# A token-mixing kernel: one PSUM tile for the transposition of x, chunks that enter over seven steps, and final channel mixes at other places

## The chip, the cores and the metric

The kernel runs on one core of a Trainium2 chip. The metric is the time of one execution on the device in microseconds (us). The core has five engines that work side by side, each in the order of its own instructions: TensorE (PE) for matmuls, VectorE (DVE), ScalarE (ACT), GpSimd (POOL), and SyncE (SP), which here only issues DMAs. ACT and POOL issue DMAs too. SBUF is the working memory, PSUM the memory into which PE writes.

## The reference

Two layers follow each other. The inputs are x (8 batches, 4224 tokens, 192 channels, float32), eight sets of seven taps, two token-mixing matrices of 4224 x 4224 and two channel-mixing matrices of 192 x 192.

```python
# layer 1: a causal convolution over 7 tokens, its taps softmaxed, one set per group of 24 channels
w = softmax(weight)                                  # [8 heads, 7 taps]
x = einsum('hk,bskhg->bshg', w, windows_of_7(x))     # [8, 4224, 192]

# layer 2
theta = x @ w_theta
zr, zi = x * cos(theta), x * sin(theta)
y = einsum('ts,bsd->btd', w_tok_r, zr) + einsum('ts,bsd->btd', w_tok_i, zi)
u = x + y
return u + maximum(u @ w_ch, 0)
```

By far the most work is y: two products of a 4224 x 4224 matrix with 4224 x 1536 numbers (8 batches of 192 channels).

## The kernel before

**Chunks and token blocks.** The 4224 source tokens are cut into 33 chunks k of 128, the 4224 target tokens into 33 blocks tb of 128. A unit is a pair of blocks (the seventeenth unit is a single block). For a pair the two products are done by a scheme of seven runs (`runs`, L394) on sums and differences of the matrices (S1 to S4) and of zr and zi (Z11, T1, Z21, Z22, T2, T4, T3). A run is two matmuls per chunk (L427). The sums of the matrices are formed by DVE (`turn`, L325, transposes the tiles that arrive from DRAM; `wsum`, L333). After a run `give` (L383) adds the result from PSUM to the row buffers `pv` of the unit; this is done by DVE (L392), and in the first pass by ACT for four of the seven (L390). The PSUM tiles of the runs (`y`) have two buffers.

**Steps.** SBUF holds eleven chunks (`zpool`). A step t treats one unit with all chunks that are there. A chunk stays for 17 steps, so that it meets each unit once; then a new chunk takes its place one step later. `base` (L64) says in which step each of the eleven slots begins, `start` (L66) the step in which each chunk begins. As slots begin at different steps, a step has between 2 and 11 chunks (`n`); one step is 0.324 x n x 7 us of PE work (`time`, L300), 24.9 us for a pair with eleven chunks. Between passes the sums are kept in DRAM (`part`): SP loads them into `pv` (`load_rows`, L356; six buffers shared with the input of chunks) and stores them at the end of the step (L440).

**What makes a chunk.** `Chunk.tasks` (L255): two convolutions as matmuls (`conv`, L192) evacuated by ACT; the transposition of x by PE in two halves of six 128 x 128 transposes (`transpose`, L221, `transposed`, L157), each into one bank of a PSUM tile of two banks, evacuated to the SBUF tile `uT` by ACT or DVE; two theta products with sine and cosine by ACT (`theta`, L229); products and sums by DVE. Convolutions, transposes and thetas share two PSUM tiles of two banks (`banks`, L109). The first eleven chunks are made in a loop at the start (L645 to L689), in which `between(n)` puts up to n pairs of token-mixing matmuls between the tasks, as far as their chunks are ready. The later ones are made within steps: each task has a place in units of a seventh of a step (`pos`, L528), the second chunk of one step begins 2.3 units after the first.

**The end.** In the last 17 steps (`final`) each block is finished: `add_x` (L367) has added x before (POOL, L374, or a DMA that accumulates in DRAM, L379, for the late steps and the first two of the final ones), ACT casts u to half precision (`cast`, L444), u is transposed, and `output` (L461) does the channel mix on PE (eight matmuls for a half of the columns, L138), takes the maximum and adds on DVE (L464), and stores the result (SP, L469). In final steps with all eleven chunks ("full") the transposition is a DMA on ACT's queue (`cross_u`, L458, L155). In those with fewer ("late") it is done by PE (`turn_u`, L453). `outputs` (L474) lists at which time after the end of its step, in us of token-mixing work, each of these is put into the order.

**Order.** The order on PE, DVE, ACT and POOL is written out by hand: the events of a step are sorted by their place and issued when `mix` (L414) gets there, and the helpers `pe`, `dve`, `act`, `pool` keep each engine to that order. SP's DMAs, and POOL's that are not wrapped in `pool`, are placed by a scheduler.

Of the kernel before, what the change touches and what calls it, by code (L numbers as in the profile page):

```python
# [16 lines left out]
def kernel(  # L17
# [23 lines left out]
    nc = tc.nc  # L41
# [3 lines left out]
    P = nc.NUM_PARTITIONS  # L45
# [11 lines left out]
    NG = B // GB  # L57
    GC = GB * D
# [2 lines left out]
    NW = 11  # L61
    PC = 512

    base = [0, 0, 1, 1, 2, 3, 3, 4, 4, 5, 5]  # L64
    assert len(base) == NW
    start = [base[k % NW] + (NU + 1) * (k // NW) for k in range(NK)]  # L66
    NSTEP = start[-1] + NU
# [13 lines left out]
    def pe(ins):  # L81
        return in_order("pe", ins)

    def dve(ins):
        return in_order("dve", ins)
# [58 lines left out]
    def evacuate(out, in_, by_dve=False):  # L144
        if by_dve:
            dve(nc.vector.tensor_copy(out=out, in_=in_))
        else:
            act(nc.scalar.activation(out=out, in_=in_, func=AT.Copy))  # L148

    def turned():  # L150
        return wk.tile([P, 12, P], F16, name="uT", tag="uT")
# [2 lines left out]

        act(nc.scalar.dma_start(out=uT, in_=u, transpose=True))  # L155

    def transposed(uT, u, by_dve=False):  # L157
        tp = banks("tp", F16)
        for k in range(6):
            pe(nc.tensor.transpose(  # L160
                tp[:, 0, k * P : (k + 1) * P], u[:, k * P : (k + 1) * P], ident
            ))
        evacuate(uT.rearrange("p k s -> p (k s)"), tp[:, 0, 0 : 6 * P], by_dve)

    Z11, T1, Z21, Z22, T2, T4, T3 = range(7)

    class Chunk:
# [50 lines left out]
                        out=xs[t0 : t0 + Q, :], in_=self.x[a * Q : (a + 1) * Q, :]  # L218
                    )

        def transpose(self, g):  # L221
            if g == 0:
                self.xT = turned()
            transposed(
                self.xT[:, 6 * g : 6 * g + 6, :], self.x[:, g * GC : (g + 1) * GC],
                0 < self.k < 3 or (self.k, g) == (0, 1),
            )

        def theta(self, g):  # L229
            v = channel_mix(self.xT[:, 6 * g : 6 * g + 6, :], wth).rearrange(  # L230
# [24 lines left out]
        def tasks(self):  # L255

            for j in range(2):
                yield lambda j=j: self.conv(j)
            for g in range(NG):
                yield lambda g=g: self.transpose(g)  # L260
            for g in range(NG):
                yield lambda g=g: self.theta(g)
            yield lambda: self.product(Z11)
            yield lambda: self.product(Z21)
            yield lambda: self.sums(0)
            yield lambda: self.sums(1)
# [13 lines left out]
    class Step:  # L280
# [170 lines left out]
            ))  # L451

        def turn_u(self, i, g):  # L453
            transposed(
                self.uT[i][:, 6 * g : 6 * g + 6, :], self.ub[i][:, g * GC : (g + 1) * GC]
            )

        def cross_u(self, i):  # L458
            crossed(self.uT[i], self.ub[i])
# [14 lines left out]
        def outputs(self):  # L474

            found = []
            for i in range(len(self.tbs)):
                if not self.late:
                    at = (4 if i else 0.9 - self.time / 7) if self.pair else 0.7
                    for g in range(NG):  # L480
                        found.append((at + g, lambda i=i, g=g: self.cast(i, g)))
                        found.append((at + 10.5 + 2.8 * g,
                                      lambda i=i, g=g: self.output(i, g)))
                    found.append((at + 2, lambda i=i: self.cross_u(i)))
                    continue
                at = 1.2 if i or not self.pair else 0.6 - self.time / 7
                every, turn, mix = 2.0, 1.2, 3.6
                for g in range(NG):
                    found.append((at, lambda i=i, g=g: self.cast(i, g)))
                    found.append((at + turn, lambda i=i, g=g: self.turn_u(i, g)))  # L490
                    found.append((at + mix, lambda i=i, g=g: self.output(i, g)))
                    at += every
            return found
# [7 lines left out]
    def step_events(t):  # L501
        found = []
        s = steps[t]
        if t + 1 < NSTEP:
            found += steps[t + 1].w_tasks()
            found.append((1.6, steps[t + 1].load_rows))
            if not steps[t + 1].ahead:
                for i in steps[t + 1].adds:
                    found.append((3.3 + 1.7 * i, lambda i=i: steps[t + 1].add_x(i)))
        for s in steps[t:]:  # L510
            if s.ahead and t == s.t - (4 if s.late else 10):
                for i in s.adds:
                    found.append((3.3 + 1.7 * i, lambda s=s, i=i: s.add_x(i)))
        if t + 2 < NSTEP:
            nxt = steps[t + 2]
            for m in (1, 2):
                found.append((1.3 + 3 * (m - 1), lambda m=m: nxt.load_w(m)))
        for at, f in outputs:
            begin = at - sum(s.time for s in steps[:t])
            if 0 <= begin < steps[t].time:  # L520
                found.append((7 * begin / steps[t].time, f))
        if t >= NU - 2:
            new = [k for k in range(NK) if start[k] == t + 2 and k >= NW]
            for k in new:
                found.append((4.5, lambda k=k: load_chunk(k)))
            at = 0.1
            for k in (k for k in range(NK) if start[k] == t + 1 and k >= NW):
                pos = [0, .5, 1.3, 1.6, 2.1, 2.5, 3.1, 3.15, 3.4, 3.6]  # L528

                def add(at, j, k):  # L530
                    def go():
                        if j == 0:
                            chunks[k].todo = chunks[k].tasks()
                        next(chunks[k].todo)()
                    found.append((at, go))
                for j, p in enumerate(pos):
                    add(at + p, j, k)
                at += 2.3
        return found
# [105 lines left out]
    for i in range(NW + 2):  # L645
        ch = chunks.get(i) if i < NW else None
        old = chunks[i - 1] if 0 < i <= NW else None

        def between(n):
            left = more(n)  # L650
            if 0 < i < 3:
                idle(min(left, 2))

        if ch:
            ch.conv(0)
        between(2)
        if old:
            old.theta(0)
        between(1)
        if ch:  # L660
            ch.conv(1)
        if i == 0:
            idle(4)
        ready[0] = i - 2
        between(2)
        if old:
            old.theta(1)
        if i == 1:
            for _, f in steps[0].w_tasks():
                f()  # L670
        if i + 3 < NW:
            load_chunk(i + 3)
        between(1)
        if ch:
            ch.transpose(0)
        if old:
            old.product(Z11)
        between(1)
        if ch:
            ch.transpose(1)  # L680
        if old:
            old.product(Z21)
        between(1)
        if old:
            old.sums(0)
        between(1)
        if old:
            old.sums(1)
        between(1)  # L689
    nc.vector.memset(wch[:, 1:3, :], 0.0)  # L690
    for rows, i, part_w in channel_pieces(moe_w_ch):
        nc.gpsimd.dma_start(out=wch[rows, i, :], in_=part_w)
    ready[0] = NK
# [33 lines left out]
```

## Time and profile before

| what | value |
|---|---|
| median of 5 runs | 1480.63 us |
| the five runs | 1466.3, 1472.12, 1480.63, 1482.14, 1494.6 us |
| the profiled execution: its time, its span | 1477.73 us, 1476.0 us |
| granted TensorE clock, mean | 0.991 |
| L427, token-mixing matmuls | 7656, 1292.8 us |
| L138, channel-mixing matmuls (theta and output) | 1056, 109.9 us |
| L160, transposes of x and of u on PE | 396 and 108, 42.0 us |
| L148, ACT evacuations of transposes | 79, 814 ns each |
| L392, DVE additions | 324, 951 ns each |
| L155, DMA transposes of u | 24, issue to landing 3.2 to 25.7 us, median 6.8 |
| DMA, mean over the span | 191 GB/s |

The span is the time from the first to the last instruction of the profiled execution. A group of instructions is named by its line, its engine, and what it writes and reads (`v<-wch,uT`). Busy time is the sum over its instructions; idle time in front of a group is given with what ended it. The chain that ended last is followed back from the end, from each piece of work to what released it. Busy times of engines overlap, so they do not add up to the span.

### The profile page before, as it was taken

Reading aid. Unit: us, or ns where it says so; the run is one execution under the profiler, and the core shown is the slowest. Engines: PE = TensorE matmul, PEld = TensorE weight load, DVE = VectorE, ACT = ScalarE, POOL = GpSimd, SP = SyncE. Lnnn points to the kernel's source line nnn. Section 1 sums busy time; section 2 is a strip of 40 time slices with the busy share of each in tenths; the row PEclk is TensorE's granted clock in tenths of the full one; section 3 lists DMA queues with packets and bytes.
Section 4 is the critical chain, followed back from the end, with each engine's and each line's share of the span. In section 5 each row is a group of like instructions: output and inputs, shape, how many; then the busy total and the mean of one; then the engine's idle time right before and its main releaser. Section 6 shows DMA issues by size and latency. Waiting matters only on the chain.

```text
span 1476.0 us, 23773 instructions
## 1 busy us (share of the span) xinstructions
PE 1421.2 (96%) x9807; PEld 887.2 (60%) x9807; DVE 1016.6 (69%) x1050; ACT 322.8 (22%) x413; POOL 434.8 (29%) x655
## 2 busy tenths in 40 slices
PE   7889999999999999999999999999999999996997
PEld 4556666666666666656656566666656666664665
DVE  6884554555458687777767758768778787774675
ACT  6861111111134353000000005245001101100034
POOL 7422211111223322522413333332123123233210
PEclk9999999999999999999999999999999999998999
DMA  9976756464699999987977799999898989999983
GB/s 176 225 161 145 143 100 147 94 150 92 156 225 229 213 214 274 205 224 163 244 166 215 173 196 240 187 240 262 152 201 191 212 195 239 207 249 154 246 219 118
DMA packets 272029, 281.98 MB, mean 191 GB/s; under 512 B 106673, under 2 KB 240177, under 8 KB 271921
## 3 DMA queue, kind: packets, MB, share of 16 engines
q0 software_dynamic: 162464, 92.15, 47.5%
q1 hardware_dynamic: 71824, 178.88, 34.7%
q10 hardware_dynamic: 37632, 9.44, 5.0%
q8 instruction: 77, 1.26, 0.3%
q14 instruction: 32, 0.25, 0.1%
HBM read 245.49 MB, written 108.13 MB: 240 GB/s over the span
## 4 chain that ended last, share of the span: by engine, by line
PE 84%; DVE 6%; DMA 4%; ACT 3%; issue 2%; POOL 0%; DVEq 0%; SPq 0%; ACTq 0%
PE y L427 75%; PE v L138 5%; DMA uT<-ub 3%; DVE wt L339 2%; PE pc L200 2%; ACT z L240 2%; DVE pv L392 1%; PE tp L160 1%; DVE wt L327 1%; DVE z L251 1%; DVE z L245 1%; ACT uT L148 1%; DVE pv L464 1%; ACT pv L390 0%; DMA xw<-in_x_dram 0%
## 5 line engine op out<-in xcount | busy, mean ns | idle before, releaser
L427 PE MATMUL y<-z,wt 128*128 128x384 f16 x7656 | 1292.8, 327 | 12.8 <-DVE pv L392 11.9
L427 PEld LDWEIGHTS <-wt 128*128 128x128 f16 x7656 | 740.7, 98 | 489.7 <-issue 16.4
L392 DVE TENSOR_TENSOR pv<-y,pv 128x768 f32<-128x768 f32 x324 | 308.1, 951 | 306.4 <-PE y L427 267.1
L327 DVE STREAM_TRANSPOSE wt<-st 128x1408 f16<-128x1408 f16 (+7 forms) x224 | 327.5, 1464 | 44.1 <-PE y L427 36.2
L314 POOL DMA_DIRECT2D st<-in_moe_w_tok_i_dram x232 | 132.4, 579 | 510.1 <-DVE wt L327 495.3
L314 POOL DMA_DIRECT2D st<-in_moe_w_tok_r_dram x232 | 132.5, 580 | 455.3 <-DVE wt L327 441.8
L339 DVE TENSOR_TENSOR wt<-wt 128x1408 f16<-128x1408 f16 (+7 forms) x216 | 218.5, 1012 | 45.6 <-PE y L427 43.4
L148 ACT ACTIVATE z<-pc 128x768 f16<-128x768 f32 x65 | 52.8, 813 | 390.5 <-PE pc L200 390.5
L449 ACT ACTIVATE ub<-pv 128x768 f16<-128x768 f32 x66 | 52.5, 836 | 361.3 <-DVE pv L392 321.6
L138 PEld LDWEIGHTS <-uT 128*128 128x128 f16 x1056 | 91.5, 98 | 40.7 <-DMA uT<-ub 17.3
L390 ACT ACTIVATE pv<-y 128x768 f32<-128x768 f32 x66 | 53.6, 813 | 282.8 <-PE y L427 282.7
L464 DVE SCALAR_TENSOR_TENSOR pv<-v,pv 128x768 f32<-128x768 f32 x66 | 62.7, 951 | 34.1 <-PE v L138 32.1
L187 POOL DMA_DIRECT2D xw<-in_x_dram x132 | 76.2, 587 | 29.7 <-DMA xw<-xw 5.9
L374 POOL TENSOR_TENSOR pv<-pv,xr 128x1536 f32<-128x1536 f32 x24 | 74.8, 3116 | 10.1 <-issue 9.3
L148 ACT ACTIVATE uT<-tp 128x768 f16<-128x768 f16 x79 | 63.0, 814 | 63.1 <-PE tp L160 62.2
L251 DVE TENSOR_TENSOR z<-z 128x768 f16<-128x768 f16 x132 | 73.3, 555 | 3.8
L138 PE MATMUL v<-wch,uT 128*128 128x192 f16 x528 | 54.9, 248 | 17.4 <-DMA uT<-ub 15.5
L240 ACT ACTIVATE z<-v,half_pi 128x768 f16<-128x768 f32 x66 | 59.5, 901 | 43.0 <-PE v L138 42.7
L245 DVE TENSOR_TENSOR z<-z 128x1536 f16<-128x1536 f16 x66 | 60.3, 948 | 9.9 <-ACT z L240 9.9
L138 PE MATMUL v<-wth,uT 128*128 128x192 f16 x528 | 55.0, 248 | 3.0 <-ACT z L240 2.8
L240 ACT ACTIVATE z<-v 128x768 f16<-128x768 f32 x66 | 53.1, 805 | 0.0
L160 PE MATMUL tp<-ident,z 128*128 128x128 f16 x396 | 33.1, 220 | 8.5 <-ACT z L240 8.0
(43 smaller groups left out, 147.4 us busy)
## 6 DMA issues: line engine op xcount, KB each, us to landing
part<-pv SPq DMA_DIRECT2D x79, 768.0 KB, 4.1
pv<-part SPq DMA_DIRECT2D x79, 768.0 KB, 5.8
out_dram<-pv SPq DMA_DIRECT2D x66, 384.0 KB, 5.5
st<-in_moe_w_tok_r_dram POOLq DMA_DIRECT2D x136, 176.0 KB, 5.5
st<-in_moe_w_tok_i_dram POOLq DMA_DIRECT2D x136, 176.0 KB, 5.0
xs<-z SPq DMA_DIRECT2D x132, 96.0 KB, 4.4
xw<-in_x_dram POOLq DMA_DIRECT2D x121, 96.0 KB, 5.9
xr<-xs SPq DMA_DIRECT2D x24, 384.0 KB, 4.6
```

What stands on the lines that cost most here:

```text
L138: pe(nc.tensor.matmul(v[:, k, b * D : (b + 1) * D], lhsT=tT[:, 3 * k + b + i, :], rhs=w[:, 2 * b + i, :], start=(i == 0), stop=(i == 1),))
L148: act(nc.scalar.activation(out=out, in_=in_, func=AT.Copy))
L187: nc.gpsimd.dma_start(out=self.xw[lo : lo + n, h, :, :], in_=x[:, t0 : t0 + n, :].rearrange("b s d -> s b d"),)
L240: act(nc.scalar.activation(**args))
L245: dve(nc.vector.tensor_tensor(out=o, in0=xv, in1=o, op=ALU.mult))
L251: dve(nc.vector.tensor_tensor(out=z[:, o, :], in0=z[:, a, :], in1=z[:, b, :], op=ALU.subtract))
L314: pool(nc.gpsimd.dma_start(out=st[a * Q : (a + 1) * Q, 0:nb, :, 0:n] .rearrange("i r bt s -> i (r bt) s"), in_=w[self.tbs[0] * P : (self.t ...
L327: dve(nc.vector.transpose(self.w[name][:, 0 : self.n, :, :], self.st[int(name[1])][:, int(name[0]) - 1, :, 0 : self.n * Q] .rearrange("p b ...
L339: dve(nc.vector.tensor_tensor(out=self.w[name][:, 0 : self.n, :, :], in0=self.w[a][:, 0 : self.n, :, :], in1=self.w[b][:, 0 : self.n, :, : ...
L392: dve(nc.vector.tensor_tensor(out=o, in0=yv, in1=o, op=ALU.add))
L427: pe(nc.tensor.matmul(y[cn][:, q, 0:BH], lhsT=self.w[wn][:, c, :, :].rearrange("p bt i -> p (bt i)"), rhs=chunks[k].z[:, zn, q * BH : (q + ...
L464: dve(nc.vector.scalar_tensor_tensor(out=ub, in0=channel_mix(self.uT[i][:, 6 * g : 6 * g + 6, :], wch), scalar=0.0, in1=ub, op0=ALU.max, o ...
```

## The change

Four things are changed.

1. `base` goes from `[0, 0, 1, 1, 2, 3, 3, 4, 4, 5, 5]` to `[0, 0, 1, 2, 2, 3, 4, 4, 5, 6, 6]`: the eleven slots begin in steps 0 to 6 in place of 0 to 5. There are 59 steps in place of 58. The steps at the start have 2, 3, 5, 6, 8, 9 and 11 chunks in place of 2, 4, 5, 7, 9 and 11; those at the end have 9, 8, 6, 5, 3 and 2 in place of 9, 7, 6, 4 and 2. There are six late steps in place of five, and eleven full final ones in place of twelve.
2. `transposed` takes a list of halves. For x all twelve transposes go into both banks of one PSUM tile, and one instruction evacuates 1536 columns; `transpose` is one task and not two, and `pos` has nine places in place of ten. Chunks 0 to 2 are evacuated by DVE, the others by ACT. For u it is still one half at a time.
3. In full final steps the channel mixes stand at 12, 14.7, 17.5 and 20.2 us after the end of the step, where they stood at 7.8, 10.6, 14.5 and 17.3. The cast of the second block is put at 1 in place of 4.
4. The memset of the middle of `wch` stands in DVE's written order.

```diff
@@ -61,7 +61,7 @@
     NW = 11
     PC = 512
 
-    base = [0, 0, 1, 1, 2, 3, 3, 4, 4, 5, 5]
+    base = [0, 0, 1, 2, 2, 3, 4, 4, 5, 6, 6]
     assert len(base) == NW
     start = [base[k % NW] + (NU + 1) * (k // NW) for k in range(NK)]
     NSTEP = start[-1] + NU
@@ -154,13 +154,20 @@
 
         act(nc.scalar.dma_start(out=uT, in_=u, transpose=True))
 
-    def transposed(uT, u, by_dve=False):
+    def transposed(uT, u, gs, by_dve=False):
+
         tp = banks("tp", F16)
-        for k in range(6):
-            pe(nc.tensor.transpose(
-                tp[:, 0, k * P : (k + 1) * P], u[:, k * P : (k + 1) * P], ident
-            ))
-        evacuate(uT.rearrange("p k s -> p (k s)"), tp[:, 0, 0 : 6 * P], by_dve)
+        for g in gs:
+            for k in range(6):
+                pe(nc.tensor.transpose(
+                    tp[:, g, k * P : (k + 1) * P],
+                    u[:, g * GC + k * P : g * GC + (k + 1) * P], ident,
+                ))
+        g = slice(gs[0], gs[-1] + 1)
+        evacuate(
+            uT[:, :, :].rearrange("p (g k) s -> p g (k s)", g=NG)[:, g, :],
+            tp[:, g, 0 : 6 * P], by_dve,
+        )
 
     Z11, T1, Z21, Z22, T2, T4, T3 = range(7)
 
@@ -218,13 +225,9 @@
                         out=xs[t0 : t0 + Q, :], in_=self.x[a * Q : (a + 1) * Q, :]
                     )
 
-        def transpose(self, g):
-            if g == 0:
-                self.xT = turned()
-            transposed(
-                self.xT[:, 6 * g : 6 * g + 6, :], self.x[:, g * GC : (g + 1) * GC],
-                0 < self.k < 3 or (self.k, g) == (0, 1),
-            )
+        def transpose(self):
+            self.xT = turned()
+            transposed(self.xT, self.x, range(NG), self.k < 3)
 
         def theta(self, g):
             v = channel_mix(self.xT[:, 6 * g : 6 * g + 6, :], wth).rearrange(
@@ -256,8 +259,7 @@
 
             for j in range(2):
                 yield lambda j=j: self.conv(j)
-            for g in range(NG):
-                yield lambda g=g: self.transpose(g)
+            yield self.transpose
             for g in range(NG):
                 yield lambda g=g: self.theta(g)
             yield lambda: self.product(Z11)
@@ -451,9 +453,7 @@
             ))
 
         def turn_u(self, i, g):
-            transposed(
-                self.uT[i][:, 6 * g : 6 * g + 6, :], self.ub[i][:, g * GC : (g + 1) * GC]
-            )
+            transposed(self.uT[i], self.ub[i], [g])
 
         def cross_u(self, i):
             crossed(self.uT[i], self.ub[i])
@@ -476,10 +476,10 @@
             found = []
             for i in range(len(self.tbs)):
                 if not self.late:
-                    at = (4 if i else 0.9 - self.time / 7) if self.pair else 0.7
+                    at = 1 if i or not self.pair else 0.9 - self.time / 7
                     for g in range(NG):
                         found.append((at + g, lambda i=i, g=g: self.cast(i, g)))
-                        found.append((at + 10.5 + 2.8 * g,
+                        found.append((12 + 5.5 * i + 2.7 * g,
                                       lambda i=i, g=g: self.output(i, g)))
                     found.append((at + 2, lambda i=i: self.cross_u(i)))
                     continue
@@ -525,7 +525,7 @@
                 found.append((4.5, lambda k=k: load_chunk(k)))
             at = 0.1
             for k in (k for k in range(NK) if start[k] == t + 1 and k >= NW):
-                pos = [0, .5, 1.3, 1.6, 2.1, 2.5, 3.1, 3.15, 3.4, 3.6]
+                pos = [0, .5, 1.4, 2.2, 2.6, 3.1, 3.15, 3.4, 3.6]
 
                 def add(at, j, k):
                     def go():
@@ -672,12 +672,10 @@
             load_chunk(i + 3)
         between(1)
         if ch:
-            ch.transpose(0)
+            ch.transpose()
         if old:
             old.product(Z11)
-        between(1)
-        if ch:
-            ch.transpose(1)
+        between(2)
         if old:
             old.product(Z21)
         between(1)
@@ -687,7 +685,7 @@
         if old:
             old.sums(1)
         between(1)
-    nc.vector.memset(wch[:, 1:3, :], 0.0)
+    dve(nc.vector.memset(wch[:, 1:3, :], 0.0))
     for rows, i, part_w in channel_pieces(moe_w_ch):
         nc.gpsimd.dma_start(out=wch[rows, i, :], in_=part_w)
     ready[0] = NK
```

## The prediction

> **What bounds it.** I read the page first: how busy each engine is, and which lines make up the chain that ended last.
>
> ```profile
> span 1476.0 us, 23773 instructions
> ...
> PE 1421.2 (96%) x9807; PEld 887.2 (60%) x9807; DVE 1016.6 (69%) x1050; ACT 322.8 (22%) x413; POOL 434.8 (29%) x655
> ...
> PE 84%; DVE 6%; DMA 4%; ACT 3%; issue 2%; POOL 0%; DVEq 0%; SPq 0%; ACTq 0%
> ```
>
> TensorE (PE) is the bound: it is busy for 1421.2 of 1476.0 us, so at most 55 us can be won without taking away matmuls. The change leaves the 7656 token-mixing matmuls (L427) as they are. So I looked for the 55 us. The table of stretches of 25 us shows PE full from 125 us to 1050 us but for about 0.8 us here and there; the holes are at the start (0 to 110 us, about 23 us), in the twelve full final steps (1053 to 1385 us) and after 1450 us (8 us, until the last output has landed). Next came the waits of PE in the two stages that matter, the start (first pair) and the full final steps (second pair). The columns are the total in us, how often, and the longest.
>
> ```profile
> PE tp L160 <- ACT z L240: 8.0, 10, 1.1
> ...
> PE y L427 <- DVE pv L392: 5.5, 4, 1.8
> ```
>
> ```profile
> PE v L138 <- DMA uT<-ub: 15.5, 4, 11.4
> PE y L427 <- DVE pv L392: 0.7, 2, 0.3
> ```
>
> In the final steps almost the whole loss is PE waiting in front of a channel mix (L138) for the DMA transpose of u (L155). The timeline shows the longest of these waits, and a short one:
>
> ```profile
> 1093.79 0.83 PE L138 MATMUL v<-wch,uT 128*128 128x192 f16 x8 [2.24 <-DMA uT<-ub]
> 1094.46 4.44 PE L427 MATMUL y<-z,wt 128*128 128x384 f16 x16
> ...
> 1338.59 1.76 POOL L379 DMA_DIRECT2D part<-xs  x2
> 1338.78 1.47 ACTq L155 DMA_TRANSPOSE uT<-ub  x1
> ...
> 1342.36 14.54 ACTq L155 DMA_TRANSPOSE uT<-ub  x1
> ...
> 1359.25 1.46 PE L138 MATMUL v<-wch,uT 128*128 128x192 f16 x8 [11.40 <-DMA uT<-ub]
> 1360.51 4.61 PE L427 MATMUL y<-z,wt 128*128 128x384 f16 x16
> ```
>
> Three things are to be seen. The first mix comes about 8.7 us after its transpose was issued (1054.83 to 1063.57 us where nothing waits), and usually that is enough; here it took 20.5 us, in company with an accumulating DMA issued 0.2 us before. The four waits are 2.24, 1.10, 0.80 and 11.40 us. And after two of them PE is slow: 16 matmuls take 4.44 and 4.61 us where the same 16 take 2.76 (granted clock 0.66 and 0.58 over 5 us), and the mix itself 1.46 for 0.82. With these tails the transposes cost 15.5 + 1.7 + 1.9 + 0.6 = 19.7 us of this execution.
>
> **Later mixes.** The mixes of the first token block move from 7.84 and 10.64 us of PE work into the next step to 12 and 14.7, those of the second from 14.5 and 17.3 to 17.5 and 20.2. In PE's order that is 26 matmuls more ahead of the first mix (250 in place of 224 before the first one of all), 26 x 0.163 = 4.2 us (0.163 from the chain's 1938 matmuls in 315.10 us). The casts and the transposes do not start sooner: ACT is in order and idle there (its casts wait 280 us in all for DVE's additions, L392), so it already casts the second block as soon as its sum is there, and the smaller due time changes nothing. So each wait shrinks by 4.2 us: 2.24, 1.10 and 0.80 go, 11.40 becomes 7.2, and the slow matmuls after the 2.24 go with it. That is 4.1 + 4.2 + 1.7 = **10.0 us**. The slow stretch after a wait of 7.2 us stays.
>
> The row for the clock is that 2.24 us of waiting was enough for a slow stretch, and 1.10 was not. The Trainium skill (TensorE: Matmul & The Clock Gate, What's actually happening) has the clock halved after an idle window of about 3.4 us, on a free-running window; by it the 2.24 us would have cost nothing more, and the sum here would be 8.3.
>
> What the later mixes hold up: the row buffers (pv, six) are given back 3 to 4 us later, and on SP's queue the load of rows three steps ahead stands behind each store. The load for (step 52, block 1) was issued at 1317.89 us and takes 5.8 us by its group's median; the Pool addition that needs it ran at 1335.54, so 11.8 us are free, and 3.4 are used. I cost it at nothing. If a store takes 8 us longer than here, the addition is late, and up to 3.4 us pass to PE in each of the steps with such additions, about ten additions in all. uT has two buffers: the next cast comes 22 us into the step, when the first block's is free since 14.7.
>
> **Seven entry steps.** The number of steps goes from 58 to 59, the matmuls stay. DVE gets one step more: 7 additions x 0.951 us, and the fixed part of 4 turns and 4 sums (0.16 each, from 431 ns at 256 columns against 1634 at 1408): 8 us of 1016, beside PE in the middle, where DVE is busy 17 to 21 of 25 us. SP gets two more stores and loads of 768 KB, also beside it. One block pair more falls among the late steps (n < 11), which transpose on PE: 24 transposes more, 12 in 0.91 to 1.0 us by the rows, so **+2.0 us** on PE; and two accumulating pairs (L379) take the place of two Pool additions. A step of three chunks is new, at the start and at the end. The last one has 42 x 0.163 + 4 x 0.82 + 2.0 = 12.1 us of PE work against 7 x 0.951 + 2 x 0.43 + 4 x 0.951 = 11.3 of DVE. A run of three chunks takes 0.98 us and an addition 0.95, and the run after next writes the bank that it reads. The trace has no step of three. Its bounds are nothing, and for the two such steps 7 waits of 1.8 each (the longest L427 wait for L392), 25 us. In the step of four at 1430 us the row shows hardly a wait, so I take **+1.5**, and keep both ends.
>
> **One transposition tile.** In the start-up loop (25 to 100 us) ACT is busy 61.7 of 75 us, DVE 61.3, PE 61.3: a loop of all three. The second half transpose waits for the bank that the second theta leaves, 8.0 us in ten waits. In the new order all 12 stand behind a bank that ACT emptied earlier, and that wait goes. What is late next is ACT: its evacuation of 1536 columns takes the place of two that run back to back in 1.52 us. Between no gain and the 0.2 us that the fixed part of an ACT row suggests (249 ns at 56 columns, 813 at 768, so 1421 at 1536), that is 0 to 2 us; but 14 copies (L390) fall inside the loop where 12 did, +1.6. The Trainium skill (ScalarE: Activation LUTs, What ACT_TABLE_LOAD costs) gives 186 ns + 0.833 per column and says that neighbours overlap by 93 ns; that is an estimate of 1466 ns against 1.52, hardly a gain, and with it the loop would be won by PE alone. What PE gains can be counted in its order: 182 token matmuls stand before the 22nd theta where 158 did, as step 1 no longer waits for chunk 3. If the loop keeps its length these 24 are 24 x 0.163 = 3.9 us of later work done in the holes. Bounds: a loss of 3.9 (the loop grows by them) and a gain of 8; I take **-3**. In the entry steps later on, PE stays full: the 12 transposes and 0.8 of a seventh of a step (2.3 us) cover the evacuation; only in the short step 41 (11.7 us) about 0.3 us is uncovered for each of two chunks, **+0.5**. The memset of wch goes into DVE's order behind the start-up, where only two small loads wait for it (0.2 us, beside other work).
>
> **Sum.** -10.0 + 2.0 + 1.5 - 3 + 0.5 = -9.0 us: the profiled execution, 1477.73 us with a span of 1476.0, would be 1468.7. It lies 2.9 under the median, 1480.63. The runs spread from 1466.3 to 1494.6; without any transposition wait this one would be 1477.7 - 19.7 = 1458, so the slower runs have more of that to lose, and I do not add the 2.9: **1469 us**.
>
> **Rivals.** *Waits gone altogether* (0.18): if the accumulating DMA and the transposes no longer fall together, since Pool's work depends on stores that move by 3 us, the other 9.7 go too: 1459, with 1454 to 1463. For it: eight of twelve steps have no wait at all. Against it: step 51 has the same two additions and two accumulations in Pool's order as before.
>
> *Cover that covers nothing* (0.22): the landing is set by what else is on the queues (DMA share 1.0 to 1.2 from 1275 to 1400 us), and the stores, loads and two more accumulations move along with the mixes. Then the first item is 0 and the rest -9.0 + 10.0 = +1: 1479, with 1475 to 1486. For it: after 1342 us two transposes took until 1359 together, far beyond 4.2 us. Against it: three of four waits are under 2.3 us.
>
> *Small steps bound by the additions* (0.12), the slower case: in the two steps of three chunks each run waits for the addition two runs before it, 7 x 1.8 x 2 = 25 us. With -9.0 - 1.5 for the rest: 1477.7 + 14.7 = 1492, with 1486 to 1500. It decides against the change from 10.5 us on, 0.75 us a run. For it: DVE would be 94% busy in the last of them, with outputs and turns queued ahead of additions. Against it: outputs of the step before fill PE there.
>
> **Numbers.** The forecast, 1469 (1463 to 1475 on its own), has 0.48. The range leaves out the ends of the first and last rival: 1457 to 1487. A measurement here tells from no change about 1%, 14.8 us, so faster means under 1465.8: the first rival and a third of the forecast, 0.18 + 0.16 = 0.34. Slower is over 1495.4: 0.06. Within 1%: 0.60.
>
> **What would show it.** In the changed kernel: PE's waits for uT in the full final steps fall from 15.5 to about 7 us, in one wait, not four, with a slow stretch after one; the first mix stands 12.9 us behind its transpose; the wait of the transposes for the theta evacuations (8.0 us) is gone; the first convolution after the start-up, at 424.3 us now, comes at 424.3 - 11.3 - 3 = 410 (11.3 us of token work fall behind it); 132 transposes of u on PE in place of 108. I am wrong if waits for uT stay at 15 us or more, if waits of L427 for additions exceed 10 us at either end, or if PE waits at the start for something else.

## The result, and the profile after

The changed kernel takes 1466.28 us (median of 51 runs, 1457.5 to 1479.83) against 1474.19 us (median of 91 runs, 1460.51 to 1494.81). The medians are 7.9 us apart. The ratio of the comparison is 0.9966, with a 95% interval of 0.995 to 0.9982, or 5.0 us. It leaves out runs more than 1.5% above the fastest of their kernel, most of which are runs of the kernel before, and so it is nearer to 1 than the medians. The forecast was 1469 us, with a change of under 1%.

The profiled execution of the changed kernel took 1474.28 us, 8.0 us above its kernel's median (that of the kernel before, 1477.73 us, lies 3.5 above its own). First the head of its page and the chain that ended last:

```profile
span 1472.6 us, 23807 instructions
...
PE 1423.6 (97%) x9833; PEld 889.7 (60%) x9833; DVE 1022.3 (69%) x1063; ACT 321.0 (22%) x386; POOL 437.1 (30%) x665
...
PE 82%; DVE 8%; DMA 5%; ACT 2%; issue 1%; ACTq 1%; POOL 0%; SPq 0%; DVEq 0%; POOLq 0%
```

PE has 26 matmuls more (24 transposes and two fillers at the start), DVE 6 us more work, ACT 27 instructions fewer. The bound is the same. PE's waits in the full final steps (total in us, how often, the longest):

```profile
PE v L138 <- DMA uT<-ub: 11.1, 3, 7.7
PE y L429 <- DVE pv L394: 0.3, 1, 0.3
```

The waits for the DMA transposes are 11.1 us, where the profile of before had 15.5. What is left lies in two steps. Here is the first of them in the timeline, POOL, ACT's queue and PE alone (start, duration, line; in brackets the idle time before and what ended it):

```profile
1246.78 3.69 POOL L376 TENSOR_TENSOR pv<-pv,xr 128x1536 f32<-128x1536 f32 x1 [3.02 <-issue]
...
1250.42 1.72 POOL L381 DMA_DIRECT2D part<-xs  x2
...
1258.00 1.76 POOL L381 DMA_DIRECT2D part<-xs  x2
...
1261.77 6.14 ACTq L155 DMA_TRANSPOSE uT<-ub  x1
...
1269.63 3.33 ACTq L155 DMA_TRANSPOSE uT<-ub  x1
...
1271.46 1.76 POOL L381 DMA_DIRECT2D part<-xs  x2
...
1274.84 0.82 PE L138 MATMUL v<-wch,uT 128*128 128x192 f16 x8
...
1289.54 1.46 PE L138 MATMUL v<-wch,uT 128*128 128x192 f16 x8 [7.69 <-DMA uT<-ub]
```

The first block's mix is no longer late (it ran at 1274.84 us; its transpose was issued at 1261.77, 3.8 us behind a pair of accumulating DMAs). It is now the second block's transpose, issued at 1269.63 us with an accumulating DMA 2 us behind it, that takes 20 us. At the start, the first convolution of the second pass comes at 411.05 us, where it came at 424.27. Of these 13.2 us, 11.3 are token mixing that the new steps put behind it; 1.9 are won.

### The profile page after: what moved, and what is told of

Read it like the earlier page. It is cut to its first block, busy times and chain, and to the rows that moved or that the text cites. A ratio compares the mean times of both kernels' runs of the same rounds, so it can differ in the third digit from the quotient of the medians.

```text
span 1472.6 us, 23807 instructions
## 1 busy us (share of the span) xinstructions
PE 1423.6 (97%) x9833; PEld 889.7 (60%) x9833; DVE 1022.3 (69%) x1063; ACT 321.0 (22%) x386; POOL 437.1 (30%) x665
## 4 chain that ended last, share of the span: by engine, by line
PE 82%; DVE 8%; DMA 5%; ACT 2%; issue 1%; ACTq 1%; POOL 0%; SPq 0%; DVEq 0%; POOLq 0%
PE y L429 74%; PE v L138 5%; DMA uT<-ub 3%; DVE pv L394 2%; DVE wt L341 2%; PE pc L207 2%; PE tp L162 2%; DVE z L254 1%; ACT z L243 1%; DVE z L248 1%; ACTq L155 1%; DVE wt L329 1%; DMA xs<-z 1%; DVE pv L464 1%; ACT uT L148 0%
## 5 line engine op out<-in xcount | busy, mean ns | idle before, releaser
L429 PE MATMUL y<-z,wt 128*128 128x384 f16 x7656 | 1288.6, 327 | 16.8 <-DVE pv L394 13.9
L429 PEld LDWEIGHTS <-wt 128*128 128x128 f16 x7656 | 741.3, 98 | 497.6 <-issue 22.3
L394 DVE TENSOR_TENSOR pv<-y,pv 128x768 f32<-128x768 f32 x331 | 314.9, 952 | 309.2 <-PE y L429 271.1
L392 ACT ACTIVATE pv<-y 128x768 f32<-128x768 f32 x66 | 53.5, 814 | 272.7 <-PE y L429 272.7
L148 ACT ACTIVATE uT<-tp 128x1536 f16<-128x1536 f16 (+1 forms) x52 | 61.2, 1181 | 72.5 <-PE tp L162 70.6
L376 POOL TENSOR_TENSOR pv<-pv,xr 128x1536 f32<-128x1536 f32 x22 | 69.2, 3146 | 22.0 <-DMA xr<-xs 13.2
L138 PE MATMUL v<-wch,uT 128*128 128x192 f16 x528 | 54.8, 248 | 14.6 <-DMA uT<-ub 11.1
L248 DVE TENSOR_TENSOR z<-z 128x1536 f16<-128x1536 f16 x66 | 60.4, 949 | 11.1 <-ACT z L243 11.1
L207 PE MATMUL pc<-xw,bands 96*64 96x192 f16 x528 | 36.1, 261 | 3.1 <-DMA xw<-in_x_dram 1.8
```

The source lines that it names most:

```text
L138: pe(nc.tensor.matmul(v[:, k, b * D : (b + 1) * D], lhsT=tT[:, 3 * k + b + i, :], rhs=w[:, 2 * b + i, :], start=(i == 0), stop=(i == 1),))
L248: dve(nc.vector.tensor_tensor(out=o, in0=xv, in1=o, op=ALU.mult))
L394: dve(nc.vector.tensor_tensor(out=o, in0=yv, in1=o, op=ALU.add))
L429: pe(nc.tensor.matmul(y[cn][:, q, 0:BH], lhsT=self.w[wn][:, c, :, :].rearrange("p bt i -> p (bt i)"), rhs=chunks[k].z[:, zn, q * BH : (q + ...
```

## The experiments

Each ratio is to the kernel before, timed side by side on the same chip; 0.001 is 1.5 us. The four groups of experiments ran on four chips, so between groups, and against the two medians above, ratios are safer to compare than medians. Four kernels first take the change apart.

**The mixes' places alone.**

```diff
# in the kernel before
-                    at = (4 if i else 0.9 - self.time / 7) if self.pair else 0.7
+                    at = 1 if i or not self.pair else 0.9 - self.time / 7
-                        found.append((at + 10.5 + 2.8 * g,
+                        found.append((12 + 5.5 * i + 2.7 * g,
```

> The kernel before with one edit, the later places of the channel mixes (and the cast of the second block at 1). Theory of the prediction: this alone wins 8 to 10 us (ratio to before 0.993 to 0.9945); the waits of PE for uT in the full final steps fall from 15.5 us to about 7, and the start-up is unchanged (first convolution after the start-up at 424 us). Rival 'cover that covers nothing': the landings move along, waits for uT stay at 15 us or more, ratio 0.999 to 1.001. Rival 'the gain of the whole comes from the start-up': ratio 0.998 to 1.0 here too.

Measured: 1465.58 us, ratio 0.9951 (0.9919 to 0.9984), 7.2 us less. The waits for uT in its profile are three, of 11.0 us in all; the first convolution of the second pass is at 425.1 us. So the later places win by themselves, a little less than the 8 to 10 us expected, and the waits fell to 11.0 us where about 7 was expected. The transposes were hardly quicker: the slowest landing took 22.0 us (25.7 before). "Cover that covers nothing" is out, as its 0.999 lies beyond the interval.

**All but the places.** The changed kernel with the two lines of `outputs` as they were.

> The changed kernel with the channel mixes at the places of before: seven entry steps and the one transposition tile, not the later mixes. Theory of the prediction: -3 at the start, +2.0 for 24 more transposes, +1.5 for the steps of three, +0.5: about +1 us, ratio 0.999 to 1.002. Rival 'the gain comes from the start-up': 0.994 to 0.996. Rival 'small steps bound by the additions': 1.005 or more. First convolution after the start-up at 410 to 411 us in all of them but the last, where it is at 415 or more.

Measured: 1483.73 us, ratio 1.0028 (0.9986 to 1.007), with the convolution at 412.37 us, where 410 to 411 was expected, and 18.4 us of waits for uT in the profile. Against the whole change the places are worth 0.0062, or 9.1 us. The interval holds the expected 0.999 to 1.002, but the middle is above it.

**The seven steps alone.** In the kernel before only `base` is changed.

> The kernel before with one edit, the seven entry steps. Theory of the prediction: +2.0 and +1.5 at the end, -2 at the start by the 24 token matmuls that find room in the loop: +1.5 us, ratio 1.000 to 1.002. If the steps of three chunks are bound by the additions: 1.005 or more, with waits of L427 for L392 of over 10 us in the first 130 or the last 80 us. If the start-up loop gains more than was counted: 0.997 or less.

Measured: 1483.93 us, ratio 1.0066 (1.0025 to 1.0106): 9.7 us more, where 1.5 was expected. But the waits that were named for this case are not there: L427 waits for L392 for 7.6 us in the first 130 us (5.5 before) and 1.3 us at the end (0.4 before). The convolution is at 413.70, which with the 11.3 us is 0.7 us later than before, not 2 sooner. Nor did the waits for uT grow: 14.4 us in this profile, 15.5 before. So this profile does not show where most of the cost lies.

**The one transposition tile alone.** In the kernel before only `transposed`, `transpose`, `tasks`, `pos`, the start-up loop and the place of the memset are changed.

> The kernel before with one edit, the twelve transposes of x into one tile of two banks with one evacuation. Theory of the prediction: the wait of the transposes for the theta evacuations (8.0 us) goes, but the loop is held by ACT too, so that 1 us is won, ratio 0.998 to 1.000. If the loop was held by that wait: -5 to -8 us, 0.9945 to 0.997. If the longer burst and the later theta cost more than they win: over 1.001.

Measured: 1473.21 us, ratio 0.9979 (0.994 to 1.0018), which can't tell 1 us from 5. The start of the trace can: the convolution comes at 419.01 us, 5.3 us sooner than before, with the same steps. (The three profiles with the tile and six steps at the start have it at 419.0 to 420.4 us, the four with neither part at 424.3 to 425.1.) The start-up loop of this kernel, 25 to 100 us (length, then PE, weight loads, DVE, ACT and POOL busy, granted clock, DMA share, GB/s):

```profile
25.00:100.00 75.00, 66.24 (x596) 43.95 (x593) 66.04 (x98) 62.31 (x77) 31.20 (x55) 0.98 1.12 220
```

and the same stretch of the kernel before:

```profile
25.00:100.00 75.00, 61.27 (x557) 40.02 (x555) 61.29 (x91) 61.68 (x83) 29.27 (x52) 0.98 1.04 208
```

PE and DVE do 5 us more work in the same time, ACT hardly more. Engines were not the limit of the loop; the wait of the second half transpose was. The merged evacuation takes 1458 ns, where a pair took 1.52 us, so the evacuation itself gives next to nothing. That is also near the 1466 ns that the prediction worked out from the Trainium skill (ScalarE: Activation LUTs, What ACT_TABLE_LOAD costs).

**Without the accumulating DMAs.** What makes the transposes late? Here those DMAs are left out, in both kernels. x is then missing from the late steps' sums; all else is done.

```diff
     def add_x(self, i):
...
-            for cols in (slice(0, HN), slice(HN, N)):
-                pool(nc.gpsimd.dma_start(
-                    out=part[(self.t // NU - 1) % 2][self.tbs[i], :, cols],
-                    in_=xs[rows, cols], accum_op=ALU.add,
-                ))
+            return
```

> The kernel before without the accumulating DMAs (L379): x is left out of the sum in the nine blocks of the late steps, all else is done. Theory: those DMAs are what makes the transposes of steps 49 to 51 late, so three of the four waits for uT (1.10, 0.80, 11.40 us) go with their slow stretch, and only waits like the 2.24 of step 43 stay: 8 to 15 us less, ratio 0.990 to 0.9945. Rival, the transposes are late by themselves or by the loads and stores: waits for uT stay at 10 us or more, ratio 0.998 to 1.0.

> The changed kernel without the accumulating DMAs (L381): x is left out of the sum in the eleven blocks of the late steps, all else is done. Theory: the remaining waits for uT (11.1 us, all in steps 50 to 52) go altogether; ratio to before 0.987 to 0.991, the same time as the kernel before without those DMAs, or 2 to 4 us less. Rival: waits for uT stay, ratio 0.994 to 0.997.

Measured: 1458.23 us for the kernel before (0.9898, 0.9861 to 0.9935) and 1459.0 for the changed one (0.9895, 0.9858 to 0.9931). The kernel before still has four short waits in the profile, all ahead of 1236 us, so none in the steps from 49 on:

```profile
PE v L138 <- DMA uT<-ub: 5.8, 4, 1.8
```

The changed one has none at all. The slowest landing of a transpose falls from 25.7 to 9.8 us, and from 19.9 to 9.9. For the kernel before, with and without these DMAs (least, median, longest):

```profile
DMA to landing us min/median/max: 3.2/6.8/25.7
```

```profile
DMA to landing us min/median/max: 3.2/6.0/9.8
```

So the accumulating DMAs are behind the long waits: they cost the kernel before 16.0 us in the medians, and the changed kernel 7.3 (15.0 and 10.5 us by the ratios). And with them gone the whole change is worth nothing: all else in it adds up to +0.8 us, less than these runs can tell from no difference. Of the two outcomes expected for the changed kernel, the same time as the other or 2 to 4 us less, it is the first.

**Accumulating DMAs ten steps ahead.**

```diff
# in the changed kernel
-            if s.ahead and t == s.t - (4 if s.late else 10):
+            if s.ahead and t == s.t - 10:
```

> The changed kernel with the accumulating DMAs of the late steps ten steps ahead in place of four: they fall in steps 43 to 48, not 49 to 54. If they make the transposes late wherever they are, the waits for uT move to steps 43 to 48 and the time stays (0.994 to 0.998). If it is the particular meeting in steps 49 to 52, where two Pool additions and two accumulations stand in one step, the waits shrink to under 4 us: 0.988 to 0.992.

Measured: 1487.56 us, ratio 1.0082 (1.0046 to 1.0118). Worse, beyond both expectations. The waits for uT are six, of 14.8 us, between 1144 and 1311 us, where in the changed kernel none comes before 1289 us; and L429 waits 4.6 us for L394. Seven of the ten Pool additions of the last pass stand in steps 43 to 48, so the accumulations now share a step with additions in five steps of six. Four of the six waits move with the DMAs, as the first theory had it. That sharing a step with additions makes them worse fits, but this kernel alone does not show it. The last two waits, 2.2 and 0.4 us, fit no theory here:

```profile
1249.90 1.70 POOL L381 DMA_DIRECT2D part<-xs  x2
...
1286.58 2.29 ACTq L155 DMA_TRANSPOSE uT<-ub  x1
...
1290.60 9.81 ACTq L155 DMA_TRANSPOSE uT<-ub  x1
...
1302.04 1.46 PE L138 MATMUL v<-wch,uT 128*128 128x192 f16 x8 [2.22 <-DMA uT<-ub]
```

These two transposes landed 15.4 and 20.4 us after their issue, and the last accumulating DMA had landed at 1258.1 us, 28 us before the first of them. In flight beside them were matrix loads, a load of rows and stores of outputs. So a landing can be long without an accumulating DMA in flight.

**Mixes later still.**

```diff
# in the changed kernel
-                        found.append((12 + 5.5 * i + 2.7 * g,
+                        found.append(((12 if self.t + 1 < NSTEP and steps[self.t + 1].late else 16) + 5.5 * i + 2.7 * g,
```

> The changed kernel with the channel mixes 4 us later still (16, 18.7, 21.5 and 24.2 us after the end of the step) in all full final steps but the last, which keeps its places. If the cover is what counts, each wait left shrinks by another 4 us: a wait of 7.7 to 3.7, one of 3 to 0, so that 4 to 7 us are won against the changed kernel: 0.989 to 0.993. If later mixes hold up the row buffers, waits of L429 for L394 appear in the final steps, and it is 0.996 or more.

Measured: 1460.3 us, ratio 0.9899 (0.9853 to 0.9944): 6.0 us under the changed kernel's median (9.9 by the ratios). There is no wait for uT left, where 3.7 us were expected to stay. The row buffers hold nothing up: L429 waits 0.3 us for L394 in the final steps, as in the changed kernel. But it is not shown that the 4 us of cover did this. The landings of this profile are short:

```profile
DMA to landing us min/median/max: 3.2/7.2/12.8
```

The first blocks' transposes landed within 9.6 us, the second blocks' within 12.8. Where nothing waits, the changed kernel's profile has its mixes 11.1 to 13.1 and 14.8 to 16.6 us behind the issue; there, too, none of these would have been late. The accumulating DMAs are all there, and some are in flight beside the transposes. Why the landings are short, and whether the moved mixes have to do with it, is open.

**Six steps, the tile, mixes later still.** The parts that win, without the one that loses.

> Six entry steps as before, the one transposition tile, and the channel mixes at 16, 18.7, 21.5 and 24.2 us (the last full step at 12 to 20.2). Theory now: the tile alone is worth 5 to 6 us at the start, the seven steps cost about 7 us with it, and 4 us more of cover hide what is left of the waits. Then 1458 (the kernel before without accumulating DMAs) less 5.7: 1451 to 1454 us, ratio 0.984 to 0.987, and faster than the changed kernel and than its variant with the mixes 4 us later. If the seven steps cost nothing of their own, it is no faster than that variant: 0.989 to 0.991.

Measured: 1454.13 us, ratio 0.9863 (0.9835 to 0.9891), 20 us less than before; the fastest kernel of this study. It is 6.2 us under the same with seven steps (0.0036 by the ratios, 5.3 us). As in neither PE waits for uT, this is what the seven steps cost by themselves when the tile is there. The landings are short here as well, 10.9 us at most. PE's waits from 1000 to 1400 us, the short step ahead of the final ones included, where the first two stand:

```profile
PE v L138 <- ACT uT L148: 0.6, 2, 0.3
PE v L138 <- ACT z L243: 0.5, 1, 0.5
PE y L429 <- DVE pv L394: 0.3, 1, 0.3
```

**Seven steps in the last pass only.**

```diff
# in the kernel with the tile alone
-    start = [base[k % NW] + (NU + 1) * (k // NW) for k in range(NK)]
+    last_pass = [0, 0, 1, 2, 2, 3, 4, 4, 5, 6, 6]
+    start = [(last_pass if k >= 2 * NW else base)[k % NW] + (NU + 1) * (k // NW)
+             for k in range(NK)]
```

> The one transposition tile and the mixes' places of before, with six entry steps in the first two passes and seven in the last alone. Theory now: of the 7 us between the tile with six steps (ratio 0.998) and the tile with seven (1.003) about half is lost at the start; here the start keeps its gain (token matmuls before the first chunk of the second pass end as with the tile alone, that convolution at 419 us), and the end costs 2.0 for 24 transposes, 1 for the step of three, and some waiting for uT: ratio 1.000 to 1.0015. If all of the 7 us comes from the end: 1.003 again.

Measured: 1485.5 us, ratio 1.0056 (1.0021 to 1.009). The convolution is at 420.42 us, so the start keeps its gain, as expected; with seven steps there as well it is at 412.37 + 11.3 = 423.7. But the time, above what was expected, is no better than with seven steps throughout (the intervals overlap), and the waits for uT are 21.5 us in a profile that lies 5.5 us above its kernel's median. So the trace shows that seven steps lose 3 us at the start on top of the tile; that the rest is lost in the waits at the end is not shown. POOL shows one thing that the steps change there. In this kernel (step 49 begins at about 1238 us):

```profile
1244.98 2.30 POOL L318 DMA_DIRECT2D st<-in_moe_w_tok_r_dram  x4 [8.12 <-DVE wt L331]
1247.29 3.10 POOL L378 TENSOR_TENSOR pv<-pv,xr 128x1536 f32<-128x1536 f32 x1
1250.33 1.75 POOL L383 DMA_DIRECT2D part<-xs  x2
1260.58 2.35 POOL L318 DMA_DIRECT2D st<-in_moe_w_tok_i_dram  x4 [8.49 <-DVE wt L331]
1262.91 1.76 POOL L383 DMA_DIRECT2D part<-xs  x2
```

and in the kernel before (step 49 begins at about 1254 us):

```profile
1235.60 3.18 POOL L374 TENSOR_TENSOR pv<-pv,xr 128x1536 f32<-128x1536 f32 x1
...
1260.97 2.28 POOL L314 DMA_DIRECT2D st<-in_moe_w_tok_r_dram  x4 [11.37 <-DVE wt L327]
1263.23 1.77 POOL L379 DMA_DIRECT2D part<-xs  x2
1274.00 2.35 POOL L314 DMA_DIRECT2D st<-in_moe_w_tok_i_dram  x4 [9.00 <-DVE wt L327]
1276.34 1.76 POOL L379 DMA_DIRECT2D part<-xs  x2
```

With 59 steps each unit comes one step later, but the first late step is still step 53, and so the accumulations still begin in step 49. The last of a group of Pool additions has moved into that step (the 1247.29 row; before it stood in step 48, at 1235.60). It stands ahead of the first accumulation, and the second one is issued just ahead of the transposes: 1262.91 and 1266 us here, 1276.34 and 1281.26 before. In the profiles with seven steps and the old places the two waits behind this meeting are 2.9 and 3.6 us (steps alone) and 2.7 and 6.2 us (here); before, it was 1.10. In the kernel with all but the places it was only 0.8, though the addition stands in step 49 there too; so the meeting does not cost the same in each execution, and the addition alone does not decide it. What goes with the cost is the distance. In six profiles, two of them with seven steps, the pair of accumulations ahead of these transposes was issued 4.9 to 6.0 us before the first of them, and they landed 4.8 to 10.3 us after their issue. In three, all with seven steps at the end (changed kernel, steps alone, this one), it was 2.9 to 3.8 us, and they took 11.7 to 12.3 us for the first block and 16.4 to 19.9 for the second. These are nine single executions, not an experiment.

**Accumulating DMAs in the middle of their step.** The last two kernels, one with six steps and one with seven, move them off the transposes without taking any away.

```diff
# in the kernel before, and in the changed kernel with the old places of the mixes
             if s.ahead and t == s.t - (4 if s.late else 10):
                 for i in s.adds:
-                    found.append((3.3 + 1.7 * i, lambda s=s, i=i: s.add_x(i)))
+                    found.append((2.5 + 0.8 * i, lambda s=s, i=i: s.add_x(i)))
```

> The kernel before with the accumulating DMAs of the late steps at 2.5 and 3.3 sevenths of their steps in place of 3.3 and 5.0, so that both stand in Pool's order between the two matrix loads, some 10 to 13 us into the step, after the transposes of one step and well before those of the next. Theory: it is the meeting in time with the transposes that makes them late, so most of the waits for uT go (15.5 us to under 6) and the time falls to 1460 to 1465, ratio 0.990 to 0.994. If the accumulating DMAs burden the queues wherever they stand in the step: 0.998 to 1.002.

> The changed kernel with the mixes' places of before and the accumulating DMAs at 2.5 and 3.3. With seven steps the Pool addition for step 50 stands in step 49, in which the accumulations begin; with six it stood a step sooner. Theory: this second shared step, next to the one before step 52, is what the seven steps cost, by pushing accumulations to the transposes; with the accumulations early in the step it matters less, and 1462 to 1468 comes out, ratio 0.991 to 0.996, against 1.003 with the accumulations late. If the seven steps cost their 7 us elsewhere, this stays 4 us or more above its sibling with six steps and adds the same waits as before.

Measured: 1458.81 us with six steps, ratio 0.9905 (0.9868 to 0.9943), and 1463.79 with seven and the tile, 0.9927 (0.9896 to 0.9957). The kernel before with this one edit, its mixes where they were:

```profile
PE v L138 <- DMA uT<-ub: 2.7, 3, 1.7
PE y L427 <- DVE pv L392: 0.3, 1, 0.3
```

and its timeline around the transposes of step 49:

```profile
1261.73 3.47 POOL L379 DMA_DIRECT2D part<-xs  x4
...
1279.75 1.60 ACTq L155 DMA_TRANSPOSE uT<-ub  x1
...
1283.28 1.90 ACTq L155 DMA_TRANSPOSE uT<-ub  x1
...
1289.32 3.46 POOL L379 DMA_DIRECT2D part<-xs  x4
```

The same bytes are accumulated in the same steps, 18 us ahead of the transposes and 6 us behind them, and the time is that of the kernel without any accumulating DMA (1458.23). So for the kernel before the cause of the long waits is shown: it is when the accumulating DMAs run, not that they run. With seven steps the edit is worth 0.0101 (1.0028 to 0.9927), with six 0.0095. So moving them wins about the same with either, and the theory that they are what the seven steps cost is not borne out. The kernel with seven steps and the tile stays 5.0 us above the other in the medians (3.2 by the ratios), where the two without accumulating DMAs were 0.8 apart. That is half of the sign that was named for a cost elsewhere; the other half, the same waits as before, is not there. Its profile has 0.5 us of waits for uT, but its runs reach from 1457.47 to 1470.4 us, and the intervals overlap; whether some meeting is left in its slower executions is not settled.

## Why the prediction was right, and where it was not

**The later mixes, -10.0 us: right.** 7.2 us alone and 9.1 on top of the rest, though in the changed kernel's profile the waits fell by 4.4 us and not by 8.3. The mechanism held: with the places alone a first block's transpose that landed 15.4 us after its issue made PE wait 2.25 us, where the 8.9 us of cover of before would have left 6.5. The longest wait left is 7.7 us, where 7.2 was worked out; that the two numbers are so close is chance. It stands after step 49, not after step 51, and it belongs to the second block, whose mixes got only 3 us; the prediction had looked at the first block alone. So there are three waits, not one. In the changed kernel's profile a slow stretch follows the waits of 7.69 us (the mix in 1.46 for 0.82) and of 2.99, but not the one of 0.39, as the row of 2.24 us had suggested:

```profile
1342.82 0.87 PE L138 MATMUL v<-wch,uT 128*128 128x192 f16 x8 [2.99 <-DMA uT<-ub]
1343.49 4.44 PE L429 MATMUL y<-z,wt 128*128 128x384 f16 x16
```

All profiles of this study together have 45 waits of 0.2 us or more in front of a channel mix between 1040 and 1400 us. None of the 25 up to 1.83 us is followed by a slow stretch, seven of the nine from 2.22 to 2.99 us are, and all eleven from 3.48 us on. The rule of the Trainium skill (TensorE: Matmul & The Clock Gate, What's actually happening), with its idle window of about 3.4 us, would have let the 2.99 pass; here the measurement decides.

**What the later mixes hold up, nothing: right**, with 0.3 us of waits for the additions even 4 us later still.

**The start, -3: right in size (-1.9), wrong in its parts.** The step that failed is "what is late next is ACT", which left the tile 0 to 2 us. The tile alone wins 5.3 us, as the wait of 8.0 us was on the path and ACT was not full. And the 24 token matmuls that were counted in PE's order "as step 1 no longer waits for chunk 3" were put down to the seven steps: 12 of them come with the tile alone (170 stand before the 22nd theta there), and the steps alone win nothing (0.7 us lost). On top of the tile they take back some 3 us of its gain (in the six profiles with both, the convolution is at 421.8 to 423.7 in terms of before, against 419.0 to 420.4). More matmuls in a loop are no gain if the loop grows with them. Two errors of opposite sign met.

**The end, +2.0 and +1.5: right.** From the first transpose of u on PE to the end it is 90.0 us with the seven steps alone (90.7 in the changed kernel) and 72.6 before. Of the 17.4 us, 11.4 are token matmuls that the smaller late steps leave there (35 more products of run and chunk at 0.325 us), 3.3 the four mixes of one more pair, 2.0 the transposes. That leaves 0.7 for the step of three chunks. "Small steps bound by the additions" is out: L429 waits 1.3 us for them at the end.

**The short step, +0.5: right.** Twice 0.30 us for the evacuation show in it.

**What was costed at nothing and was not:** "two accumulating pairs (L379) take the place of two Pool additions". The number of pairs did not matter. That one addition now shares step 49 with the first accumulations was left out, though the prediction had named just such a step, 51, as the place of the 11.4 us wait. What that sharing costs is not shown. With the mixes at their old places the seven steps cost 9.7 us alone, with an interval of 3.7 to 15.6; some 3.4 us of it are fixed (0.7 at the start, 2.7 at the end). The rest is open. It is not seen as waits: in that kernel's profile, which took 5.7 us longer than the one of before, they were 14.4 us against 15.5. On top of the tile, in kernels without a wait for uT, the seven steps cost 5.3 us by the ratios, and here the fixed parts, 3 at the start and 2.7 at the end, account for it.

**The sum.** Without accumulating DMAs the two kernels differ by +0.8 us; the prediction's terms other than the waits gave +1.0. The accumulating DMAs cost 16.0 us before and 7.3 after in the medians (15.0 and 10.5 by the ratios), against 19.7 and 9.7 for all waits in the forecast, which were read from one profiled execution. The sum was -9.0; -7.9 came out in the medians and -5.0 by the ratio.

**The rivals.** "Waits gone altogether", at 1459 us, is what the kernels without waits show, and 1457.5 us is the fastest run of the changed kernel; it is an end of its spread, not its median. For "cover that covers nothing" the prediction has two transposes take until 1359 us together; only the first had landed then, at 1359.2, and the second landed at 1368.1.

What stays open: why a DMA transpose that meets accumulating DMAs takes up to 28 us (28.2 in the kernel with all but the places) in some executions and under 13 in others, and why two took 15.4 and 20.4 us without one in flight. No run changed the size of the pieces of either.

## What to carry to other kernels

When a wait ends on a DMA that is sometimes late, look at what was issued just before it on the other queues: here moving two DMAs within their step was worth as much as taking them away, and more than the whole change. More distance between issue and use covers a wait only by as much as it adds; with 8 us of it the time came out as low, but the landings were shorter as well, and why is open. A part of a change that shifts the numbering of steps moves work that no line of the diff names; list which events now share a step, and measure what that costs before blaming it.

## What was not expected of the hardware

The slowest of the 24 DMA transposes of 384 KB landed 25.7 us after its issue with accumulating DMAs about, and after 9.8 us without them; the median hardly changed (6.8 and 6.0 us). While the landing was slow, issuing the next transpose held ACT's queue for 14.5 us, where the median is 1.6 us. And two back-to-back evacuations of 768 columns by ACT take 1.52 us against 1.46 for one of 1536: merging them saved PE's wait for a bank, not ACT's time.
